# A decode layer on one core: K loaded into V's buffer, the MLP's first layer moved, and w2 read in longer rows

## The chip, the cores and the metric

The kernel runs on one core of a Trainium2 chip. The metric is the device time of one execution in microseconds (us). A run counts as fast when it lies within 1.5% of its kernel's fastest. Each experiment was timed in five rounds beside the kernel before, on the same chip. The experiments ran in three groups on three chips, with medians of the kernel before of 113.86 (e1 to e4), 113.94 (e5, e6, e7, e9) and 113.86 us (e10 to e12), so medians of different groups compare to about 0.1 us.

## The reference, cut to what matters

One token (1 x 1024) passes through a layer norm, then through two branches that are added to it: attention with 32 query heads over the last 4096 keys of 4 key/value heads, and an MLP with a second layer norm.

```python
xn = _layernorm(x)
q  = xn @ wq                          # wq: 1024 x 4096, 8.39 MB
p  = softmax(q @ k[last 4096].T / sqrt(128))   # k: 4 x 4096 x 128, 4.19 MB
a  = (p @ v[last 4096]) @ wo          # v: 4.19 MB; wo: 4096 x 1024, 8.39 MB
h  = gelu(_layernorm(xn) @ w1 + b1)   # w1: 1024 x 3584, 7.34 MB
out = x + a + h @ w2 + b2             # w2: 3584 x 1024, 7.34 MB
```

All data are bf16. Each weight is used once for one token, so 39.85 MB must come out of memory whatever the kernel does.

## The kernel before

Three buffers are used twice: `bufA` holds wq and then wo; `bufB` holds K as it is loaded and then w1; `bufKV` holds the transposed K and V, and then w2. The sync engine issues all large loads in this order, with the waits that protect the buffers:

```python
wo_sb   = bufA[...]                                   # after wq, same bytes
w1_sb   = bufB[:, :].rearrange("p (kc c) -> p kc c", kc=DC)
knat_sb = bufB[:, 0:HKV * W].rearrange(...)           # K as loaded: w1's place
kt_sb   = bufKV[:, 0:HKV * W].rearrange(...)          # K transposed
v_sb    = bufKV[:, HKV * W:2 * HKV * W].rearrange(...)
w2_sb   = bufKV[:, 0:FC * 1024].rearrange(...)        # over K^T and V
...
# sync engine
for kc in range(DC):  sync.dma_start(out=wq_sb[:, kc], ...)            # L495
for g in range(HKV):  sync.dma_start(out=knat_sb[:, g], ...)           # L497
for g in range(HKV):  sync.dma_start(out=v_sb[:, g], ...)              # L502
sync.wait_ge(s_pe, mval("pe", f"kt{HKV * NCH - 1}"))   # last K transpose
for kc in range(DC):  sync.dma_start(out=w1_sb[:, kc], ...)            # L508
sync.wait_ge(s_pe, mval("pe", "qT"))
for gi in range(8):   sync.dma_start(out=wo_sb[:, 4*gi:4*gi+4, :], ...)# L511
sync.wait_ge(s_pe, mval("pe", "oT"))                   # attention's output
...                   sync.dma_start(out=w2_sb[:, c0:c0+gsz, :], ...)  # L518
```

TensorE works in this order: q (256 pairs of weight load and matmul, L354), K transposes (L373), scores (L389), transpose of the probabilities (L401), attention's output (L419), MLP's first layer (224 pairs, L445), projection by wo (64 matmuls of 512 columns, L459 and L462), and by w2 (56 such matmuls, L471 and L475). The last two stages have one column as weights and 512 columns of wo or w2 as moving data:

```python
for c in range(4 * gi, 4 * gi + 4):
    pe.matmul(acc_lo, lhsT=oT_bf[:, c:c+1], rhs=wo_sb[:, c, 0:512],    ...)
    pe.matmul(acc_hi, lhsT=oT_bf[:, c:c+1], rhs=wo_sb[:, c, 512:1024], ...)
```

## Time and profile before

| | before |
|---|---|
| time, median | 113.98 us (16 runs, 113.37 to 114.41; 113.9 in the six runs known before predicting) |
| span of the profiled run | 112.0 us |
| read | 39.86 MB |
| longest wait of the sync queue | 28.2 us, first w1 load |
| busy shares: TensorE / VectorE / ScalarE | 62% / 25% / 17% |

Two rows of the page of the kernel before. The span is cut into 40 slices of 2.8 us; the first row is the busy share of the DMA engines in tenths (9 is 90% or more), the second what they moved.

```profile
DMA  2999999999999991199999999999999999999910
GB/s 59 422 425 427 436 424 422 419 424 422 413 422 416 419 422 50 28 364 394 425 425 423 428 386 360 400 383 396 381 386 392 380 389 389 385 388 387 332 48 1
```

The engines are full, but for a hole: the two slices at 50 and 28 GB/s. The windowed view of the kernel before gives numbers: each line is a stretch of time, its length, the busy time of each engine (with instructions), the granted clock, the DMA share and the rate.

```profile
core 0: us, PE busy (x) PEld busy (x) DVE busy (x) ACT busy (x) POOL busy (x), PEclk, DMA share, GB/s
4.00:42.00 38.00, 17.14 (x348) 14.38 (x349) 12.83 (x48) 7.86 (x14) 0.00 (x0) 1.00 1.01 422
42.00:48.50 6.50, 5.27 (x51) 3.13 (x52) 4.49 (x7) 3.77 (x7) 0.00 (x0) 1.00 0.22 71
48.50:64.00 15.50, 9.13 (x151) 5.73 (x149) 6.58 (x14) 4.70 (x5) 0.00 (x0) 0.79 1.01 418
68.00:84.00 16.00, 13.07 (x234) 8.13 (x234) 1.10 (x6) 0.23 (x1) 0.00 (x0) 0.58 1.04 387
84.00:104.00 20.00, 17.24 (x78) 6.13 (x77) 0.00 (x0) 0.00 (x0) 0.00 (x0) 1.00 1.05 387
```

From 42.0 to 48.5 us the rate is 71 GB/s in place of 422. In the last two lines, wo and w2 in rows of 2 KB, it is 387 although the DMA share is full. The waits of the sync queue of the kernel before name the hole's cause (who waited, for whom, us in total, times, longest):

```profile
SPq L508 <- PE psum L373: 28.2, 1, 28.2
```

L508 is w1, L373 the last K transpose: w1 cannot land while K lies in `bufB`.

The timeline of TensorE in the kernel before, second half, shows when its stages ran (start, length, instruction, count, and idle time before with what ended it; "issue" means that it waited for nothing the profile shows):

```profile
60.08 1.03 PE L401 MATMUL psum<-Dbf,p_sb 32*128 32x32 bf16 x32 [5.92 <-DVE Dbf L276]
61.56 3.56 PE L419 MATMUL psum<-pT_bf,bufKV 128*128 128x8 bf16 x128 [0.45 <-DVE pT_bf L278]
...
68.28 3.55 PE L445 MATMUL psum<-y2T_bf,bufB 128*128 128x1 bf16 x128 [1.28 <-issue]
74.48 2.35 PE L445 MATMUL psum<-y2T_bf,bufB 128*128 128x1 bf16 x83 [2.65 <-issue]
76.76 0.59 PE L459 MATMUL psum<-bufA,oT_bf 128*1 128x512 bf16 x1
```

TensorE stands idle for 5.9 us before L401 (softmax), then does the MLP's first layer (L445). In the w2 stage it waits for loads; from its waits after 76 us:

```profile
PE psum L471 <- DMA bufKV<-in_B_w_dram: 3.3, 5, 0.8
```

### The profile page before, as it was taken

The numbers are of one execution on the slowest core, as the hardware profiler recorded it, in microseconds if no ns is written. First come the engines' busy times: TensorE is split into PE (matmuls) and PEld (weight loads), VectorE is DVE, ScalarE is ACT, GpSimd is POOL, SyncE is SP. The second block draws the span as 40 slices with busy tenths as digits, with TensorE's granted clock in tenths as the row PEclk, the third lists the DMA queues.
The fourth block names the chain that finished last, engine by engine and source line by source line (L and its number), as shares of the span: only waits on it lengthen the run. The fifth ranks groups of instructions, "written<-read, shape, count | busy, mean of one in ns | idle before, by whom it ended". The sixth has DMA issues, their size and how long they took to land.

```text
span 112.0 us, 2144 instructions
## 1 busy us (share of the span) xinstructions
PE 69.4 (62%) x930; PEld 40.5 (36%) x930; DVE 27.7 (25%) x104; ACT 18.6 (17%) x29; POOL 0.2 (0%) x4
## 2 busy tenths in 40 slices
PE   0032000049678889699303986639999998777981
PEld 0021000049576656344003946635333333222320
DVE  3655300000027888567504000003000000000002
ACT  1201600000006677600293000000000000000002
POOL 0000000000000000000000000000000000000000
PEclk9999999999999999999975555555599999999999
DMA  2999999999999991199999999999999999999910
GB/s 59 422 425 427 436 424 422 419 424 422 413 422 416 419 422 50 28 364 394 425 425 423 428 386 360 400 383 396 381 386 392 380 389 389 385 388 387 332 48 1
DMA packets 11468, 39.99 MB, mean 357 GB/s; under 512 B 703, under 2 KB 707, under 8 KB 9412
## 3 DMA queue, kind: packets, MB, share of 16 engines
q1 hardware_dynamic: 11394, 39.85, 90.3%
q8 instruction: 7, 0.11, 0.4%
q10 hardware_dynamic: 66, 0.01, 0.1%
q14 instruction: 1, 0.01, 0.0%
HBM read 39.86 MB, written 0.00 MB: 356 GB/s over the span
## 4 chain that ended last, share of the span: by engine, by line
SPq 41%; DMA 29%; PE 15%; DVE 8%; issue 3%; ACT 1%; DVEq 0%
SPq L511 24%; DMA bufA<-in_A_wq_dram 17%; SPq L518 15%; DMA bufKV<-in_B_w_dram 12%; DVE bufKV L263 8%; PE psum L354 6%; PE psum L373 4%; PE psum L389 3%; SPq L495 3%; PE psum L471 1%; PE psum L475 1%; ACT bufKV L305 1%; ACT out_row L331 0%; ACT out_row L332 0%; DVEq L27 0%
## 5 line engine op out<-in xcount | busy, mean ns | idle before, releaser
L354 PE MATMUL psum<-xnT_bf,bufA 128*128 128x1 bf16 x256 | 7.1, 165 | 14.4 <-DMA bufA<-in_A_wq_dram 12.7
L459 PE MATMUL psum<-bufA,oT_bf 128*1 128x512 bf16 x32 | 13.6, 424 | 0.0
L305 ACT ACTIVATE bufKV<-psum 128x512 bf16<-128x512 f32 x16 | 9.6, 597 | 23.8 <-PE psum L373 23.7
L462 PE MATMUL psum<-bufA,oT_bf 128*1 128x512 bf16 x32 | 13.4, 419 | 0.0
L373 PE MATMUL psum<-I,bufB 128*128 128x128 bf16 x128 | 12.3, 246 | 1.5 <-DVE bufKV L263 0.5
L471 PE MATMUL psum<-bufKV,h_bf 128*1 128x512 bf16 x28 | 10.6, 378 | 3.4 <-DMA bufKV<-in_B_w_dram 3.3
L354 PEld LDWEIGHTS psum<-xnT_bf,bufA 128*128 128x128 bf16 x256 | 7.0, 104 | 14.5 <-issue 14.5
L263 DVE CAST bufKV<-psum 128x512 bf16<-128x512 f32 x16 | 11.1, 691 | 2.1 <-PE psum L373 0.8
L475 PE MATMUL psum<-bufKV,h_bf 128*1 128x512 bf16 x28 | 10.6, 379 | 0.0
L373 PEld LDWEIGHTS psum<-I,bufB 128*128 128x128 bf16 x128 | 8.7, 109 | 5.0 <-DVE bufKV L263 3.8
L445 PE MATMUL psum<-y2T_bf,bufB 128*128 128x1 bf16 x224 | 6.4, 165 | 3.9 <-issue 3.9
L290 DVE CAST out_row<-psum 1x256 bf16<-1x256 f32 x1 | 0.4, 411 | 30.9 <-PE psum L471 30.9
L445 PEld LDWEIGHTS psum<-y2T_bf,bufB 128*128 128x128 bf16 x224 | 6.2, 104 | 4.1 <-issue 4.1
L389 PE MATMUL psum<-bufKV,qT_pad 128*32 128x512 bf16 x32 | 7.1, 379 | 0.8 <-ACT bufKV L305 0.8
L270 DVE TENSOR_REDUCE pmax<-psum 32x1 f32<-32x512 f32 x8 | 5.4, 679 | 2.8 <-PE psum L389 2.8
L471 PEld LDWEIGHTS psum<-bufKV,h_bf 128*1 128x1 bf16 x28 | 2.3, 83 | 9.6 <-DMA bufKV<-in_B_w_dram 6.8
L331 ACT ACTIVATE out_row<-psum 1x256 bf16<-1x256 f32 x1 | 0.4, 374 | 31.6 <-PE psum L475 31.6
L256 DVE CAST qT_pad<-psum 128x8 bf16<-128x8 f32 x4 | 0.7, 166 | 20.0 <-PE psum L354 19.9
L313 ACT ACTIVATE p_sb<-psum,smw 32x2048 bf16<-32x2048 f32 x2 | 3.9, 1958 | 8.4 <-DVE smw L272 8.3
L459 PEld LDWEIGHTS psum<-bufA,oT_bf 128*1 128x1 bf16 x32 | 2.9, 91 | 5.1 <-issue 1.8
L401 PE MATMUL psum<-Dbf,p_sb 32*128 32x32 bf16 x32 | 1.0, 183 | 5.9 <-DVE Dbf L276 5.9
L462 PEld LDWEIGHTS psum<-bufA,oT_bf 128*1 128x1 bf16 x32 | 2.9, 90 | 4.9 <-issue 1.5
(74 smaller groups left out, 33.5 us busy)
## 6 DMA issues: line engine op xcount, KB each, us to landing
bufA<-in_A_wq_dram SPq DMA_DIRECT2D x8, 1024.0 KB, 12.1
bufA<-in_A_wo_dram SPq DMA_DIRECT2D x8, 1024.0 KB, 15.4
bufB<-in_B_w_dram SPq DMA_DIRECT2D x8, 896.0 KB, 10.5
bufKV<-in_B_w_dram SPq DMA_DIRECT2D x5, 1024.0 KB, 14.3
bufB<-in_A_k_cache_dram SPq DMA_DIRECT2D x4, 1024.0 KB, 24.6
bufKV<-in_A_v_cache_dram SPq DMA_DIRECT2D x4, 1024.0 KB, 28.1
bufKV<-in_B_w_dram SPq DMA_DIRECT2D x2, 768.0 KB, 13.3
bufKV<-in_B_w_dram SPq DMA_DIRECT2D x1, 512.0 KB, 12.3
```

Of the source, the lines that this page charges most:

```text
L263: lambda g=g, cb=cb, b=b: vec.tensor_copy(kt_sb[:, g, 512 * cb:512 * (cb + 1)], psum[:, SA[b]:SA[b] + 512]),
L305: lambda g=g, cb=cb, b=b: act.activation(kt_sb[:, g, 512 * cb:512 * (cb + 1)], psum[:, SA[b]:SA[b] + 512], _AF.Copy),
L354: lambda h=h, kc=kc: pe.matmul(qT_psum[:, h:h + 1], lhsT=wq_sb[:, kc, h * P:(h + 1) * P], rhs=xnT_bf[:, kc:kc + 1], start=(kc == 0), stop= ...
L373: lambda g=g, c=c, b=b, i=i: pe.matmul(psum[:, SA[b] + P * i:SA[b] + P * (i + 1)], lhsT=knat_sb[:, g, c, :], rhs=I128[:, :], start=True, s ...
L389: lambda g=g, t=t: pe.matmul(psum[0:HQ, 512 * t:512 * (t + 1)], lhsT=qT_pad[:, g, :], rhs=kt_sb[:, g, 512 * t:512 * (t + 1)], start=(g == ...
L445: lambda c=c, kc=kc, last=last: pe.matmul(hT_psum[:, c:c + 1], lhsT=w1_sb[:, kc, c * P:(c + 1) * P], rhs=y2T_bf[:, kc:kc + 1], start=False ...
L459: lambda c=c: pe.matmul(acc_lo, lhsT=oT_bf[:, c:c + 1], rhs=wo_sb[:, c, 0:512], start=False, stop=False)
L462: lambda c=c: pe.matmul(acc_hi, lhsT=oT_bf[:, c:c + 1], rhs=wo_sb[:, c, 512:1024], start=False, stop=False)
L471: lambda c=c, last=last: pe.matmul(acc_lo, lhsT=h_bf[:, c:c + 1], rhs=w2_sb[:, c, 0:512], start=False, stop=last),
L475: lambda c=c, last=last: pe.matmul(acc_hi, lhsT=h_bf[:, c:c + 1], rhs=w2_sb[:, c, 512:1024], start=False, stop=last),
L511: sync.dma_start(out=wo_sb[:, 4 * gi:4 * gi + 4, :], in_=wo_dram[:, 4 * gi:4 * gi + 4, :],).then_inc(s_wo[gi], 16)
L518: sync.dma_start(out=w2_sb[:, c0:c0 + gsz, :], in_=w2_dram[:, c0:c0 + gsz, :],).then_inc(s_w2[gi], 16)
```

## The change

The intent: close the hole, read w2 in longer rows, and fill TensorE's idle time during softmax. K goes where V will be; w1 follows K without a wait; V waits for the transposes, on GpSimd's queue. w2 (and with it w1's columns and b1) is permuted so that a partition reads four consecutive rows; the matching weights of the MLP's first layer are then read with a step of four elements. The diff, cut to its core:

```diff
-    b1_dram = B_b1.rearrange("(c p) -> c p", p=P)
+    b1_dram = B_b1.rearrange("(cc m) -> cc m", m=512)
-    w2_dram = B_w2.rearrange("(c p) n -> p c n", p=P)
+    w2_dram = B_w2.rearrange("(cc p j) n -> p cc j n", p=P, j=4)
-    W2G = [4, 4, 4, 4, 4, 3, 3, 2]
+    W2G = [4, 4, 4, 4, 2, 2, 2, 2, 2, 2]
-    knat_sb = bufB[:, 0:HKV * W].rearrange("p (g u d) -> p g u d", g=HKV, u=NU)
+    knat_sb = v_sb
+    w1_j = bufB[:, :].rearrange("p (kc cc m j) -> p kc cc m j", kc=DC, m=P, j=4)
 ... # the exp of the probabilities in three pieces (512, 1536, 2048), not two
 ... # TensorE: MLP's first layer now between the scores and the probabilities' transpose
-                        lhsT=w1_sb[:, kc, c * P:(c + 1) * P],
+                        lhsT=w1_j[:, kc, c // 4, :, c % 4],
 ... # sync engine: wq, K, then
+            for i in range(DC):
+                sync.dma_start(out=w1_sb[:, i], in_=w1_dram[:, i]).then_inc(s_w1[i], 16)
             sync.wait_ge(s_pe, mval("pe", "qT"))
 ...         # wo, then after oT: w2 in the new groups
+        @block.gpsimd
+        def _(pool):
+            pool.wait_ge(s_pe, mval("pe", f"kt{HKV * NCH - 1}"))
+            for i in range(HKV):
+                pool.dma_start(out=v_sb[:, i], in_=A_v_cache[...]).then_inc(s_v[i], 16)
```

More of the change, by code (lines that the diff above doesn't have):

```diff
@@ L107, in bass_parallel_sum__sliding_block_cached__mixer_channel_mlp__decode_kernel @@
     xb2 = sb([2, 512], bf16)
-    b1_28 = sb([FC, P], bf16)
+    b1_28 = sb([FC // 4, 512], bf16)
     J32 = sb([32, 32], bf16)
@@ L148, in bass_parallel_sum__sliding_block_cached__mixer_channel_mlp__decode_kernel @@
     s_v = [nc.alloc_semaphore(f"s_v{i}") for i in range(HKV)]
-    s_wo = [nc.alloc_semaphore(f"s_wo{i}") for i in range(HQ // 4)]
-    W2G = [4, 4, 4, 4, 4, 3, 3, 2]
+    WOG = 4
+    s_wo = [nc.alloc_semaphore(f"s_wo{i}") for i in range(HQ // WOG)]
+    W2G = [4, 4, 4, 4, 2, 2, 2, 2, 2, 2]
     s_w2 = [nc.alloc_semaphore(f"s_w2{i}") for i in range(len(W2G))]
@@ L159, in bass_parallel_sum__sliding_block_cached__mixer_channel_mlp__decode_kernel @@
     w1_sb = bufB[:, :].rearrange("p (kc c) -> p kc c", kc=DC)
-    knat_sb = bufB[:, 0:HKV * W].rearrange("p (g u d) -> p g u d", g=HKV, u=NU)
+    w1_j = bufB[:, :].rearrange("p (kc cc m j) -> p kc cc m j", kc=DC, m=P, j=4)
     kt_sb = bufKV[:, 0:HKV * W].rearrange("p (g c) -> p g c", g=HKV)
     v_sb = bufKV[:, HKV * W:2 * HKV * W].rearrange("p (g u d) -> p g u d", g=HKV, u=NU)
+    knat_sb = v_sb
     w2_sb = bufKV[:, 0:FC * 1024].rearrange("p (c n) -> p c n", c=FC)
+    w2_j = bufKV[:, 0:FC * 1024].rearrange("p (cc j n) -> p cc j n", cc=FC // 4, j=4)
     PS_XT = 3584
@@ L184, in bass_parallel_sum__sliding_block_cached__mixer_channel_mlp__decode_kernel @@
     hT_psum = psum[:, PS_HT:PS_HT + FC]
+    hT_j = hT_psum.rearrange("p (cc j) -> p cc j", j=4)
+    b1_j = b1_28[:, :].rearrange("p (m j) -> p m j", j=4)
     oT_psum = psum[:, PS_OT:PS_OT + HQ]
@@ L272, in vec_prog @@
         E.op(lambda: vec.tensor_scalar(smw[:, 1:2], smw[:, 0:1], -scale, None, _ALU.mult), name="negb")
-        E.wait("act", "exp1")
-        E.op(lambda: vec.tensor_reduce(smw[:, 2:3], esum8[:, 0:2], _AX.X, _ALU.add))
+        E.wait("act", "exp2")
+        E.op(lambda: vec.tensor_reduce(smw[:, 2:3], esum8[:, 0:3], _AX.X, _ALU.add))
         E.op(lambda: vec.reciprocal(smw[:, 3:4], smw[:, 2:3]))
@@ L310, in act_prog @@
         E.wait("dve", "negb")
-        for sx in range(2):
+        for sx, (e0, e1) in enumerate(((0, 512), (512, 2048), (2048, 4096))):
             E.op(
-                lambda sx=sx: act.activation(
-                    p_sb[:, 2048 * sx:2048 * (sx + 1)],
-                    psum[0:HQ, 2048 * sx:2048 * (sx + 1)],
+                lambda sx=sx, e0=e0, e1=e1: act.activation(
+                    p_sb[:, e0:e1],
+                    psum[0:HQ, e0:e1],
                     _AF.Exp,
@@ L347, in pe_prog @@
         E.wait("dve", "var2")
-        for kc in range(DC):
-            E.wait_sem(s_wq[kc], 16)
+        for i in range(DC):
+            E.wait_sem(s_wq[i], 16)
         for h in range(HQ):
@@ L397, in pe_prog @@
                 )
+        E.wait("act", "exp0")
+        E.wait("dve", "y2")
+        E.wait_sem(s_b1, 16)
+        for i in range(DC):
+            E.wait_sem(s_w1[i], 16)
+        for j in range(4):
+            E.op(
+                lambda j=j: pe.matmul(
+                    hT_j[:, :, j], lhsT=b1_j[:, :, j], rhs=I128[0:FC // 4, 0:FC // 4], start=(j == 0), stop=False
+                )
+            )
+        for c in range(FC):
+            for kc in range(DC):
+                last = (c == FC - 1) and (kc == DC - 1)
+                E.op(
+                    lambda c=c, kc=kc, last=last: pe.matmul(
+                        hT_psum[:, c:c + 1],
+                        lhsT=w1_j[:, kc, c // 4, :, c % 4],
+                        rhs=y2T_bf[:, kc:kc + 1],
+                        start=False,
+                        stop=last,
+                    ),
+                    name=("hT" if last else None),
+                )
         E.wait("dve", "D")
@@ L434, in pe_prog @@
             )
-        E.wait("act", "exp0")
-        E.wait("dve", "y2")
-        E.wait_sem(s_b1, 16)
-        for kc in range(DC):
-            E.wait_sem(s_w1[kc], 16)
-        E.op(lambda: pe.matmul(hT_psum, lhsT=b1_28[0:FC, :], rhs=I128[0:FC, 0:FC], start=True, stop=False))
-        for c in range(FC):
-            for kc in range(DC):
-                last = (c == FC - 1) and (kc == DC - 1)
-                E.op(
-                    lambda c=c, kc=kc, last=last: pe.matmul(
-                        hT_psum[:, c:c + 1],
-                        lhsT=w1_sb[:, kc, c * P:(c + 1) * P],
-                        rhs=y2T_bf[:, kc:kc + 1],
-                        start=False,
-                        stop=last,
-                    ),
-                    name=("hT" if last else None),
-                )
         E.wait("dve", "oTbf")
-        for gi in range(HQ // 4):
+        for gi in range(HQ // WOG):
             E.wait_sem(s_wo[gi], 16)
-            for c in range(4 * gi, 4 * gi + 4):
+            for c in range(WOG * gi, WOG * gi + WOG):
                 E.op(
@@ L493, in _ @@
         def _(sync):
-            for kc in range(DC):
-                sync.dma_start(out=wq_sb[:, kc], in_=wq_dram[:, kc]).then_inc(s_wq[kc], 16)
-            for g in range(HKV):
+            for i in range(DC):
+                sync.dma_start(out=wq_sb[:, i], in_=wq_dram[:, i]).then_inc(s_wq[i], 16)
+            for i in range(HKV):
                 sync.dma_start(
-                    out=knat_sb[:, g],
-                    in_=A_k_cache[0, g, W0:SK, :].rearrange("(q u) d -> q u d", q=P),
-                ).then_inc(s_k[g], 16)
-            for g in range(HKV):
-                sync.dma_start(
-                    out=v_sb[:, g],
-                    in_=A_v_cache[0, g, W0:SK, :].rearrange("(q u) d -> q u d", q=P),
-                ).then_inc(s_v[g], 16)
-            sync.wait_ge(s_pe, mval("pe", f"kt{HKV * NCH - 1}"))
-            for kc in range(DC):
-                sync.dma_start(out=w1_sb[:, kc], in_=w1_dram[:, kc]).then_inc(s_w1[kc], 16)
-            sync.wait_ge(s_pe, mval("pe", "qT"))
-            for gi in range(HQ // 4):
-                sync.dma_start(
-                    out=wo_sb[:, 4 * gi:4 * gi + 4, :],
-                    in_=wo_dram[:, 4 * gi:4 * gi + 4, :],
+                    out=knat_sb[:, i],
+                    in_=A_k_cache[0, i, W0:SK, :].rearrange("(q u) d -> q u d", q=P),
+                ).then_inc(s_k[i], 16)
+            for i in range(DC):
+                sync.dma_start(out=w1_sb[:, i], in_=w1_dram[:, i]).then_inc(s_w1[i], 16)
+            sync.wait_ge(s_pe, mval("pe", "qT"))
+            for gi in range(HQ // WOG):
+                sync.dma_start(
+                    out=wo_sb[:, WOG * gi:WOG * gi + WOG, :],
+                    in_=wo_dram[:, WOG * gi:WOG * gi + WOG, :],
                 ).then_inc(s_wo[gi], 16)
@@ L517, in _ @@
             for gi, gsz in enumerate(W2G):
+                cc, j = c0 // 4, c0 % 4
                 sync.dma_start(
-                    out=w2_sb[:, c0:c0 + gsz, :],
-                    in_=w2_dram[:, c0:c0 + gsz, :],
+                    out=w2_j[:, cc, j:j + gsz, :],
+                    in_=w2_dram[:, cc, j:j + gsz, :],
                 ).then_inc(s_w2[gi], 16)
@@ L526, in _ @@
             sync.wait_ge(s_out, 16)
+        @block.gpsimd
+        def _(pool):
+            pool.wait_ge(s_pe, mval("pe", f"kt{HKV * NCH - 1}"))
+            for i in range(HKV):
+                pool.dma_start(
+                    out=v_sb[:, i],
+                    in_=A_v_cache[0, i, W0:SK, :].rearrange("(q u) d -> q u d", q=P),
+                ).then_inc(s_v[i], 16)
         @block.vector
```

## The prediction

> **What bounds it now.** The kernel reads 39.85 MB; the DMA engines are the limit. The page's slices show them full except for one hole. By the windowed view the rate is 419 to 425 GB/s from 4 to 41 us (wq and K, rows of 8 KB). Between 42.0 and 48.5 us only 0.46 MB moved, 1.1 us' worth at 423 GB/s: 5.4 us are lost. The cause is in the sync queue's waits: the first w1 load waits 28.2 us for the last K transpose (46.3 us), because w1 lands in K's buffer, and nothing else was left to load. Later the rate is 421 to 427 with w1 (7 KB rows), but only 382 to 390 GB/s from 68 to 106 us, with wo and w2 in 2 KB rows, at a full DMA share. The last w2 groups land at 107.1 us; 10 matmuls of 0.215 us follow, then copies and the output, to 112.0 us. The chain of waits agrees: 41% sync queue's issues, 29% DMA.
>
> **What the change does.**
> 1. K goes to V's future place, so w1 has its buffer alone and is issued right behind K. V waits for the last transpose, on GpSimd's queue, while w1 (until about 49 us: 19.9 MB at 423 GB/s from 2.1 us) and wo (free from the q matmuls' end, 32.7 us) keep the engines busy. The hole vanishes: -5.4 us.
> 2. w2 is read in rows of 8 KB (four loads) and 4 KB (six). The Trainium skill, "DMA: Bandwidth & Descriptors", section Why small descriptors are slow, states a fixed cost per packet; the trace agrees in direction, 423 GB/s at 7 to 8 KB against 386 at 2 KB. Its 7.34 MB take about 17.6 in place of 19.0 us (estimate from these rates): -1.4 us.
> 3. Last groups of two chunks: 4 to 8 matmuls after the last landing, not 10: -0.4 to -1.2 us.
> 4. The MLP's first layer moves ahead of the probabilities' transpose and loads weights with a step of four elements (8 bytes). Its 224 pairs now cost 6.4 us plus 3.9 us of issue gaps. "SBUF — State Buffer", section Door 1, states that two hits per 16-byte line suffice; no strided weight load is in this trace. I expect 6 to 13 us, from about 56 us on.
> 5. V shares the engines with wo from 46 us; by estimate it lands at 60 to 68 us, and attention's output is ready at 68 to 72 us. Then w2 may be issued; wo keeps the engines busy until about 81 us, so some 9 us of slack cover 4 and 5.
>
> **Sum.** 113.9 - 5.4 - 1.4 - 0.8 = 106.3; plus 0.2 for two queues: 106.5 us, range 105.0 to 109.0. Chances: faster by over 2% 0.94, within 2% 0.04, slower 0.02.
>
> **What would show it.** No slice with DMA share under 9 before the tail; w1 landed at about 50 us; w2 moving above 405 GB/s; V landed before 70 us; attention's output before 78 us; last w2 landing near 100 us; under 1.8 us of matmuls after it.
>
> **What would make it wrong.** Strided loads of 100 ns or more per pair (22 us), or V starved behind the deep sync queue: attention's output after 81 us, and a new hole of several us before w2. Or the second half's rate is limited by something other than row size: then w2 gains nothing, 108 us.

## The result, and the profile after

| | before | after |
|---|---|---|
| time, median | 113.98 us (16 runs) | 106.45 us (8 runs, 106.27 to 106.70) |
| ratio | | 0.9343, 95% interval 0.9325 to 0.9362 |
| span of the profiled run | 112.0 us | 104.5 us |

Ratios are the mean time of one kernel's fast runs over that of the other's of the same rounds, so not quite the ratio of the medians quoted. All outputs are right.

The page's DMA rows of the changed kernel, slices of 2.6 us:

```profile
DMA  4999999999999999999999999999999999999910
GB/s 57 396 430 420 433 414 427 427 423 414 423 411 415 429 412 420 428 396 430 417 405 410 413 417 383 387 388 384 389 387 392 419 411 430 412 406 411 370 72 1
```

The hole is gone. The windowed view of the changed kernel (stretches chosen for the same stages; wo moves in the fourth, w2 in the fifth):

```profile
4.00:42.00 38.00, 17.15 (x348) 14.39 (x349) 12.82 (x48) 7.86 (x14) 0.00 (x0) 1.00 1.01 422
42.00:48.50 6.50, 5.27 (x51) 3.14 (x52) 4.49 (x7) 3.77 (x7) 1.86 (x4) 1.00 1.02 418
48.50:64.00 15.50, 12.62 (x229) 9.18 (x226) 5.90 (x13) 4.45 (x6) 0.36 (x1) 0.79 1.02 409
64.00:80.00 16.00, 13.83 (x216) 7.92 (x214) 1.99 (x8) 0.82 (x2) 0.00 (x0) 0.56 1.05 387
82.00:98.00 16.00, 16.00 (x76) 6.22 (x74) 0.00 (x0) 0.00 (x0) 0.00 (x0) 1.00 1.02 414
```

The second stretch went from 71 to 418 GB/s, w2 from 387 to 414; wo, whose 2 KB rows were not touched, stayed at 387. Among the sync queue's waits w1 (now L512) no longer appears. The only one left that holds back a load is wo's (L515), 3.4 us for q, with other loads in flight:

```profile
SPq L515 <- PE psum L359: 3.4, 1, 3.4
```

TensorE's timeline in the changed kernel:

```profile
56.10 0.29 PE L410 MATMUL psum<-I,b 7*128 7x7 bf16 x4 [1.94 <-ACT p_sb L318]
56.33 5.91 PE L418 MATMUL psum<-y2T_bf,bufB 128*128 128x1 bf16 x173
63.18 1.86 PE L418 MATMUL psum<-y2T_bf,bufB 128*128 128x1 bf16 x51 [0.95 <-issue]
64.97 1.03 PE L430 MATMUL psum<-Dbf,p_sb 32*128 32x32 bf16 x32
66.45 1.32 PE L448 MATMUL psum<-pT_bf,bufKV 128*128 128x8 bf16 x44 [0.45 <-DVE pT_bf L283]
...
72.74 0.59 PE L469 MATMUL psum<-bufA,oT_bf 128*1 128x512 bf16 x1
```

The MLP's first layer (L418) now fills the softmax wait, and the projections start at 72.7 us, 4 us earlier than before. TensorE's waits for w2 in the changed kernel, after 76 us, and the end of its chain of waits (start, length, what):

```profile
PEld psum L481 <- DMA bufKV<-in_B_w_dram: 1.4, 3, 0.7
PE psum L481 <- DMA bufKV<-in_B_w_dram: 0.2, 1, 0.2
```

```profile
81.04 19.90 DMA bufKV<-in_B_w_dram
100.94 0.04 issue
100.98 0.38 PE psum L481
101.36 0.22 PE psum L485
101.58 0.22 PE psum L481
101.79 0.23 PE psum L485
```

Here is the reading that the prediction had not made. The chain ends in a w2 load (100.94 us), but from 72.7 us to the end TensorE's matmuls (PE) stood idle for a load only once, for 0.2 us; its weight loads (PEld) waited three times, 1.4 us in all, mostly while earlier matmuls still ran. By the spacing of the matmuls' starts TensorE lost about 0.6 us to loads. Its 120 projection matmuls are 28 us of back-to-back work, since each takes 0.215 us, and 0.43 us for the first dozen, at half clock. So the kernel now has two limits that end within about 1 us of each other: the DMA engines, and TensorE counted from attention's output.

When a load's data are complete can be read from the trace's landing records, in which each load completes sixteen times, once per DMA engine. The last completion of some loads, in us from the span's start:

```
                     before   after
last w1 load          66.25   52.66
last V load           44.09   65.59
last wo load          89.59   83.39
last w2 load but one 107.13   99.71
last w2 load         108.41  100.94
end of span          112.0   104.5
```

The last landing moved by 7.47 us and the span by 7.5: the gain is there, ahead of the last landing.

### The profile page after: what moved, and what is told of

Its sections match the earlier page's. It is cut to its first block, busy times and chain, and to the rows that moved or that the text cites. A ratio compares the mean times of both kernels' runs of the same rounds, so it can differ in the third digit from the quotient of the medians.

```text
span 104.5 us, 2154 instructions
## 1 busy us (share of the span) xinstructions
PE 70.6 (68%) x933; PEld 42.6 (41%) x933; DVE 27.7 (26%) x104; ACT 18.9 (18%) x31; POOL 2.4 (2%) x8
## 4 chain that ended last, share of the span: by engine, by line
DMA 38%; PE 30%; SPq 12%; DVE 10%; issue 6%; ACT 2%; DVEq 0%
DMA bufKV<-in_B_w_dram 19%; DMA bufA<-in_A_wq_dram 19%; SPq L523 8%; DVE bufKV L268 8%; PE psum L418 7%; PE psum L359 7%; PE psum L394 7%; PE psum L378 4%; PE psum L448 4%; SPq L505 3%; ACT p_sb L318 1%; DVE pT_bf L283 1%; DVE pmax L275 1%; ACT bufKV L310 1%; PE psum L481 1%
## 5 line engine op out<-in xcount | busy, mean ns | idle before, releaser
L469 PE MATMUL psum<-bufA,oT_bf 128*1 128x512 bf16 x32 | 13.8, 430 | 0.0
L472 PE MATMUL psum<-bufA,oT_bf 128*1 128x512 bf16 x32 | 13.7, 427 | 0.0
L378 PE MATMUL psum<-I,bufKV 128*128 128x128 bf16 x128 | 12.3, 246 | 1.4 <-DVE bufKV L268 0.5
L378 PEld LDWEIGHTS psum<-I,bufKV 128*128 128x128 bf16 x128 | 8.7, 109 | 4.9 <-DVE bufKV L268 3.8
L418 PE MATMUL psum<-y2T_bf,bufB 128*128 128x1 bf16 x224 | 7.8, 172 | 0.9 <-issue 0.9
L418 PEld LDWEIGHTS psum<-y2T_bf,bufB 128*128 128x128 bf16 x224 | 7.6, 118 | 1.1 <-issue 1.0
L318 ACT ACTIVATE p_sb<-psum,smw 32x512 bf16<-32x512 f32 (+2 forms) x3 | 4.2, 1389 | 8.4 <-DVE smw L277 8.3
L448 PE MATMUL psum<-pT_bf,bufKV 128*128 128x8 bf16 x128 | 3.7, 168 | 2.2 <-issue 1.7
L394 PEld LDWEIGHTS psum<-bufKV,qT_pad 128*32 128x32 bf16 x32 | 3.0, 97 | 4.5 <-DVE bufKV L268 0.9
```

What stands on the lines that cost most here:

```text
L378: lambda g=g, c=c, b=b, i=i: pe.matmul(psum[:, SA[b] + P * i:SA[b] + P * (i + 1)], lhsT=knat_sb[:, g, c, :], rhs=I128[:, :], start=True, s ...
L394: lambda g=g, t=t: pe.matmul(psum[0:HQ, 512 * t:512 * (t + 1)], lhsT=qT_pad[:, g, :], rhs=kt_sb[:, g, 512 * t:512 * (t + 1)], start=(g == ...
L418: lambda c=c, kc=kc, last=last: pe.matmul(hT_psum[:, c:c + 1], lhsT=w1_j[:, kc, c // 4, :, c % 4], rhs=y2T_bf[:, kc:kc + 1], start=False, ...
L448: lambda g=g, u=u: pe.matmul(oT_psum[:, G * g:G * (g + 1)], lhsT=v_sb[:, g, u, :], rhs=pT_bf[:, HQ * u + G * g:HQ * u + G * (g + 1)], star ...
L469: lambda c=c: pe.matmul(acc_lo, lhsT=oT_bf[:, c:c + 1], rhs=wo_sb[:, c, 0:512], start=False, stop=False)
L472: lambda c=c: pe.matmul(acc_hi, lhsT=oT_bf[:, c:c + 1], rhs=wo_sb[:, c, 512:1024], start=False, stop=False)
```

## The experiments

Theory A: only the DMA engines limit; the other parts of the change ride along. Theory B: TensorE's work behind attention's output is a second limit of nearly the same length, so that moving the MLP's first layer matters. In the texts below, "Theory A" and "Theory B" are these.

| run | what | median us | ratio to before (95%) | last w2 landing us |
|---|---|---|---|---|
| changed kernel | | 106.45 | 0.9343 (0.9325, 0.9362) | 100.94 |
| e1 | buffers and order alone | 108.88 | 0.9567 (0.9535, 0.9599) | 102.18 |
| e6 | rows and groups alone | 112.50 | 0.9884 (0.9862, 0.9906) | 107.08 |
| e2 | changed, natural rows | 107.90 | 0.9487 (0.9456, 0.9517) | 102.37 |
| e3 | changed, MLP late | 110.50 | 0.9709 (0.9672, 0.9746) | 101.02 |
| e4 | changed, V on sync queue | 106.46 | 0.9361 (0.9328, 0.9394) | 100.90 |
| e10 | changed, all w2 loads 8 KB rows | 107.06 | 0.9396 (0.9373, 0.9419) | 100.70 |
| e5 | changed, projections turned round | 107.20 | 0.9419 (0.9399, 0.9439) | 102.13 |
| e7 | e5 with the MLP late | 107.35 | 0.9425 (0.9408, 0.9443) | 102.22 |
| e9 | e5 with wo in 4 KB rows | 106.88 | 0.9380 (0.9361, 0.9399) | 101.89 |
| e11 | changed, 128 idle pairs | 106.63 | 0.9346 (0.9323, 0.9370) | 101.10 |
| e12 | changed, 256 idle pairs | 107.89 | 0.9462 (0.9439, 0.9486) | 102.43 |

### e1: buffers and order alone

```diff
 # on the kernel before
-    knat_sb = bufB[...]
+    knat_sb = v_sb
 ... # w1 issued behind K without a wait; V on GpSimd's queue; all else as before
```

> Step 1 alone on the kernel before (K in V's place, w1 right behind K, V on GpSimd's queue); rows, groups and the place of the MLP's first layer stay as before. Theory A (only the DMA engines limit): the hole goes, last w2 landing at about 101.7 us, 10 matmuls after it, about 108.5 us, ratio 0.952. Theory B (TensorE's work after attention's output is a second limit of nearly the same length): the MLP's first layer, still behind attention, lets the output projections start only at 75 to 77 us; their 120 matmuls take 28 us whatever lands, so TensorE ends near 104.5 us, hardly waits for any w2 landing, and the time is 109 us or more.

The last landing fell from 108.41 to 102.18 us, by 6.2 us: that is what taking out the hole was worth at the last landing. The span fell by only 4.9 us. The answer on TensorE's waits after 76 us has no line for a load at all: with the MLP's first layer still behind attention, the projections started at 76.47 us and ran through to 104.7 us, 2.5 us past the last landing. Theory B's account holds, though the time of 108.88 us lies just under its "109 us or more"; Theory A's account falls, though its time of 108.5 us was close.

### e6: rows and groups alone

```diff
 # on the kernel before: b1, w1 and w2 permuted, W2G = [4, 4, 4, 4, 2, 2, 2, 2, 2, 2]
 # K, V, w1 in their old buffers and order; the MLP's first layer in its old place
```

> Steps 2 and 3 alone on the kernel before: permuted w1, b1 and w2 rows and the ten w2 groups, but K, V and w1 in their old buffers and order and the MLP's first layer in its old place. The hole of 5.4 us stays. w2 moves at 407 to 423 GB/s: last landing near 105.7 us in place of 107.1, 4 matmuls after it: 111.4 to 112.0 us, ratio 0.977 to 0.983. Under Theory B TensorE is close behind: the strided loads make its projections start 1.4 us later, so it should hardly wait for w2 any more.

A miss in size: ratio 0.988, not 0.977 to 0.983. The landing moved by 1.33 us as the rows' sum says, but from 108.41, not from the 107.1 us that I had read as the last landing, and the smaller groups gave nothing. The part about Theory B was a miss too: TensorE's projections started at 77.4 us, only 0.6 us later than before, and it still waited 1.9 us for w2, so it did not limit here.

### e2: the changed kernel with natural rows

```diff
-    w2_dram = B_w2.rearrange("(cc p j) n -> p cc j n", p=P, j=4)
+    w2_dram = B_w2.rearrange("(c p) n -> p c n", p=P)
-                        lhsT=w1_j[:, kc, c // 4, :, c % 4],
+                        lhsT=w1_sb[:, kc, c * P:(c + 1) * P],
 ... # b1 likewise; the ten groups stay
```

> The changed kernel with w1, b1 and w2 back in natural order: w2 in 2 KB rows (same ten groups), contiguous weight loads in the MLP's first layer. Row-size theory: w2 moves at 385 to 390 GB/s again, last landing 1.2 to 1.6 us later than 100.9, time 107.5 to 108.0, ratio 0.944 to 0.950. Rival (the rate of the second half has another cause than rows, or TensorE hides it): ratio within 0.002 of the changed kernel's 0.934. The 224 pairs at contiguous weights should take 27 to 28 ns each in place of 33.8.

The last landing is 1.43 us later, the time 1.45 us. The windowed view of e2, in the stretches where wo and then w2 move:

```profile
64.00:80.00 16.00, 13.48 (x230) 7.95 (x229) 1.99 (x8) 0.82 (x2) 0.00 (x0) 0.55 1.05 386
82.00:98.00 16.00, 16.00 (x76) 6.23 (x74) 0.00 (x0) 0.00 (x0) 0.00 (x0) 1.00 1.05 386
```

At 2 KB w2 moves at 386 GB/s, as wo does; in the changed kernel it moved at 414. The time follows the row size. The contiguous pairs took 4.77 us for 176 of them, 27.1 ns each; the strided pairs of the changed kernel, in the same place, 5.91 us for 173, or 34.2 ns by the timeline (33.8 by the chain of waits, which I had quoted). By these rates the step of four costs about 1.5 us over 224 pairs. But the stage hardly grew shorter without it. TensorE's timeline in e2:

```profile
56.73 4.77 PE L412 MATMUL psum<-y2T_bf,bufB 128*128 128x1 bf16 x176
63.85 1.44 PE L412 MATMUL psum<-y2T_bf,bufB 128*128 128x1 bf16 x48 [2.35 <-issue]
65.22 1.03 PE L424 MATMUL psum<-Dbf,p_sb 32*128 32x32 bf16 x32
```

From its first pair to the next stage it took 8.5 us, against 8.6 us with the step (56.33 to 64.97 us in the changed kernel): the faster pairs were followed by a longer "issue" wait, 2.35 us in place of 0.95. What such a wait is, the section on e5, e7 and e9 takes up.

### e3: the changed kernel with the MLP's first layer back in its old place

```diff
 # TensorE's order, in words
-  scores, MLP's first layer, probabilities' transpose, attention's output, projections
+  scores, probabilities' transpose, attention's output, MLP's first layer, projections
```

> The changed kernel with only the MLP's first layer moved back behind attention's output. My prediction gave this stage 9 us of slack (Theory A): then nothing changes, 106.5 us. Theory B: the output projections start about 3 to 5 us later (75.5 to 78 us in place of 72.7) and TensorE never waits for w2; the time rises by 2.5 to 4 us, to 109 to 110.5 us, although w2 lands at about the same time or earlier.

4.05 us slower than the changed kernel, with the last w2 load at the same time within 0.1 us. The windowed view of e3 at its end:

```profile
core 0: us, PE busy (x) PEld busy (x) DVE busy (x) ACT busy (x) POOL busy (x), PEclk, DMA share, GB/s
96.00:100.00 4.00, 4.00 (x20) 1.51 (x18) 0.00 (x0) 0.00 (x0) 0.00 (x0) 1.00 0.87 346
100.00:106.00 6.00, 6.00 (x28) 2.19 (x26) 0.17 (x1) 0.00 (x0) 0.00 (x0) 1.00 0.03 10
```

For the last 6 us the DMA engines are all but idle and TensorE busy without a gap: it started the projections at 77.58 us and ended at 106.0. Of the 9 us of slack that I gave to this stage some 0.8 us exist: a start 4.84 us later cost 4.05 us. It is worse than e1, which also has the MLP late: there the weights were contiguous and the projections started 1.1 us earlier.

### e4: V on the sync queue

```diff
-            pool.wait_ge(...kt31); pool.dma_start(out=v_sb[:, i], ...)   # GpSimd
+            sync.wait_ge(...kt31); sync.dma_start(out=v_sb[:, i], ...)   # behind w1, ahead of wo
```

> The changed kernel with V issued by the sync queue, behind w1 and ahead of wo, at the same wait for the last K transpose. If GpSimd's queue matters only by letting V be issued while something else is in flight: w1 is in flight until about 49 us, V is issued at 46.4, so no hole: 106.5 us within 0.4, V lands at about 59 to 60 us. If a separate queue is needed to keep the engines full: a hole of 1 to 3 us at 46 to 50 us and 107.5 us or more.

No difference: 106.46 us, and no hole. V landed at 61.8 us in place of 65.6, a little later than I expected. This agrees with the Trainium skill, "DMA: Bandwidth & Descriptors", section Issuing engines are not separate DMA queues: loads issued by different engines run on the same 16 DMA engines and interleave. The order of issue closed the hole, and the second queue did not add to it.

### e10: w2 in seven loads, all with 8 KB rows

```diff
-    W2G = [4, 4, 4, 4, 2, 2, 2, 2, 2, 2]
+    W2G = [4, 4, 4, 4, 4, 4, 4]
```

> The changed kernel with w2 in seven groups of four chunks, all rows 8 KB, in place of four of 8 KB and six of 4 KB. The last six groups moved at about 407 GB/s, 8 KB rows at 420: the last landing comes some 0.3 us earlier, but 8 matmuls follow it (1.7 us) in place of 4 (0.9 us). Prediction from the sum: 0.3 to 0.8 us slower, 106.8 to 107.3 us. If the smaller last groups were worth nothing: 106.2 us.

As the sum said: the last landing came 0.24 us earlier, but eight matmuls followed it, and the time rose by 0.6 us. The small last groups of the change earn their shorter rows.

### e5, e7 and e9: turned-round projections

If TensorE is a second limit, halving its projection work should make its place in the chain irrelevant, and leave room for longer rows of wo.

```diff
-  pe.matmul(acc_lo, lhsT=oT_bf[:, c:c+1], rhs=wo_sb[:, c, 0:512], ...)      # 120 matmuls of 512 columns
+  pe.matmul(accT[:, n:n+1], lhsT=wo_sb[:, c, n*P:(n+1)*P], rhs=oT_bf[:, c:c+1], ...)   # 480 pairs
+  # accT (128 x 8) is copied to bf16 and turned back by one matmul with the identity
```

> The changed kernel with the two output projections turned round: blocks of the weights are the stationary operand (480 pairs of 128x128 weights and one moving column, at the 27 to 28 ns per pair seen in the other stages, 13.4 us) in place of 120 matmuls of 512 columns (28 us); the [128 x 8] result is turned back by one small matmul. Everything else as changed. If the DMA engines and TensorE tie in the changed kernel as I read it, nothing large is gained, since the last w2 load still lands near 100.9 us: 105.8 to 106.6 us. If TensorE alone set the end: 104.5 us or less.

> The same turned-round projections, with the MLP's first layer back behind attention (the place that cost 4 us in the run before). Theory B (that cost was TensorE's 28 us behind attention's output): with only 13.4 us there the late place costs nothing, 105.8 to 106.8 us. Rival (a late MLP delays the DMA issues or something else): 109 us or more again.

> Turned-round projections, and wo read in rows of 4 KB: attention's output is computed in two halves of 64 strided columns of V (256 pairs in place of 128) and put back by four small copies. Row-size theory: wo's 8.39 MB move at about 407 in place of 388 GB/s, 1.0 us less, so 104.8 to 105.5 us. Rival (TensorE or attention's later output limits): no gain over the run with turned-round projections alone.

e7 settles the question of place: with the turned-round projections, moving the MLP late costs 0.15 us (107.35 against 107.20) in place of 4.05. So the cost of the late place was TensorE's work behind attention's output, as Theory B says. But e5 itself was 0.75 us slower than the changed kernel, a miss: its last w2 load landed at 102.13 us, 1.2 us later, though nothing about the large loads was edited. e7 missed its range for the same reason (102.22 us). e9 read wo at 408 GB/s in place of 387 and won 0.3 us over e5, less than the 1.0 us expected. Its loads were ahead of e5's by more than that up to the fifth w2 load (94.71 us against 95.82), but by only 0.24 us at the last; between 94 and 96 us they moved at 315 GB/s. Why they lost it there was not tested.

What delayed the loads? The sixteen completions of the last w2 load, each as its lead over the last one (first, eighth, fifteenth), and the times at which 16 KB packets of the instruction queue began, from the trace's landing and packet records:

```
              first   8th  15th   instruction packets at (us)
changed       -1.85 -1.35 -0.09   29.0 35.2 45.0 60.8 67.1 73.2 82.5
e5            -3.02 -2.08 -1.20   29.1 35.3 45.2 60.8 67.0 73.4 79.6 85.8 91.9 (100.4)
```

In e5 fifteen engines were done 1.2 us before the sixteenth. The load that landed at 90.8 us had no such gap (fifteenth completion 0.08 us ahead), the next, at 94.5 us, had it (1.22 us). Between them, at 91.9 us, lies the ninth instruction packet; such a packet holds an engine for 1.0 to 1.1 us. TensorE's timeline in e5 shows the other side, its waits for instructions, between runs of exactly 128 pairs (256 instructions of 64 bytes are 16 KB):

```profile
75.78 3.57 PE L463 MATMUL psum<-oT_bf,bufA 128*128 128x1 bf16 x128 [2.22 <-issue]
82.25 2.42 PE L463 MATMUL psum<-oT_bf,bufA 128*128 128x1 bf16 x85 [2.90 <-issue]
```

The Trainium skill, "Runtime: NRT & Kernel Launch", section Instruction fetch mechanics, states the 16 KiB block of 256 instructions, and calls the cost of crossing a block boundary mostly hidden. Here it was not hidden: packets came about 6.2 us apart, TensorE stood still for 2 to 3 us at a time, and one DMA engine of sixteen fell behind. The theory that the ninth packet does the harm was then tested by itself.

### e11 and e12: more instructions, nothing else

```diff
+        for _ in range(128):      # e12: 256; while TensorE waits for wq, from about 12 us
+            pe.matmul(psum[:, 3700:3701], lhsT=I128[:, :], rhs=xnT_bf[:, 0:1], start=True, stop=True)
```

> The changed kernel with 128 idle pairs (128x128 weights, one column, result unused) put on TensorE at 13 us, where it waits for wq until 23.8 us. Fetch theory (from the runs with turned-round projections): each 16 KB packet of TensorE's instructions holds one of the 16 DMA engines for 1.1 us; the first eight hit engines with slack, the ninth hits one that is already last and delays every later load by about 1.2 us. One packet more, eight in all: no change, 106.5 us within 0.3. Rival (the turned-round runs landed late because of the way TensorE reads weights): no change either.

> The same with 256 idle pairs (7 us, still inside TensorE's wait for wq): nine packets. Fetch theory: the last w2 load lands about 1.2 us later, near 102.1 us, with 15 of its 16 completions about 1.2 us ahead of the last; 107.4 to 107.9 us. Rival: no change, 106.5 us.

The instruction queue's lines on the pages of the changed kernel, e11 and e12, in this order (packets, MB, share of 16 engines' span):

```profile
q8 instruction: 7, 0.11, 0.5%
```

```profile
q8 instruction: 8, 0.13, 0.5%
```

```profile
q8 instruction: 9, 0.15, 0.6%
```

Completions of the last w2 load, and the packets, as above:

```
              first   8th  15th   instruction packets at (us)
e11           -2.06 -0.91 -0.01   17.7 30.2 36.5 45.9 62.0 68.2 74.6 83.9
e12           -3.13 -2.13 -1.46   17.2 23.3 29.9 36.1 45.7 61.8 68.2 74.6 82.8
```

Eight packets cost nothing clear of noise (106.63 us); nine cost 1.44 us (107.89 us). In e12 the ninth packet began at 82.8 us. The load that landed at 80.8 us had its fifteenth completion 0.05 us ahead of the last, the load that landed at 85.0 us 1.57 us ahead, and all later loads kept that gap to the end. The rival, that the way of reading weights delayed the loads in e5, is not needed. One reservation: the early packets also delayed wq by some 0.7 us, and with it TensorE's projections by 1.2 us. But e11 had the same delay (projections from 74.0 us, 73.9 in e12) without the gap and without the cost, the chain of waits of e12 still ends in the w2 load that landed at 102.43 us, and the gap to its other fifteen completions is direct evidence. That the ninth packet returns to an engine that has had one already fits four kernels (e5, e7, e9, e12), but the trace does not name a packet's engine, so this stays an inference.

## Why the prediction was right, and where a step was off

The forecast was 106.5 us (105.0 to 109.0) and the median 106.45. The mechanism was right: the hole and the row size gave the gain. That the sum came within 0.05 us was luck: two of its terms erred in opposite directions, and the span could follow the loads only because the MLP's first layer was moved, which the prediction had taken for a side matter (5 below).

1. *The hole, -5.4 us.* Right in cause, too small in size: 6.2 us at the last landing (e1). The lost bytes account for 5.4. After the hole the rate was slow to recover, 398 GB/s from 48.5 to 53 us, about 0.3 us by estimate. And in both kernels with the hole (before, e6) the sixteen completions of the last load were on average 1.6 us ahead of the last one, without it (after, e1) 0.9 to 1.0: the slowest engine ended some 0.6 us further behind. This gap did not come with the hole itself. In the kernel before, the last w1 load, at 66.25 us, still had its fifteenth completion 0.01 us ahead of the last; the first wo load, at 70.33 us, 1.07 us. Between them, at 65.9 us, an instruction packet began: the same sign as in e12. In e6 it is 0.09 us at 64.13 us and 1.38 at 67.70, with a packet at 65.1. So the 0.6 us may be due to where a packet fell; no run tested this.
2. *Longer rows, -1.4 us.* Right: 1.43 us (e2 against the changed kernel) and 1.33 us (e6 against before), both at the last landing. The Trainium skill's statement in "DMA: Bandwidth & Descriptors", section Why small descriptors are slow, agrees in direction, 386 to 387 GB/s at 2 KB, 408 at 4 KB (wo in e9), 418 to 422 at 7 to 8 KB.
3. *Fewer matmuls after the last landing, -0.8 us.* This term was wrong: it was worth nothing against the kernel before. The last landing before was at 108.41 us, with 4 matmuls after it, not at 107.1 with 10. I took the last wait for a load (107.1 us) as the last landing, but the next load arrived while TensorE was still busy and so left no wait. From last landing to end of span it was 3.5 us before and 3.5 after. The small groups keep their worth only against large ones with the same rows (e10, 0.6 us).
4. *Strided weights, 6 to 13 us for the stage.* Right: 8.6 us, 34 ns per pair against 27 (e2). The SBUF page's statement that two hits per 16-byte line suffice was not borne out in full: a quarter more per pair. Whether the cost arises in SBUF or in TensorE's own reading of weights, no run tells. Without the step the stage took 8.5 us (e2), since waits for instructions filled the difference.
5. *V's landing at 60 to 68 us and attention's output at 68 to 72, "some 9 us of slack cover 4 and 5".* The times were right (65.6 and 71.9 us), and for the issue of w2 there was such slack. But the slack was counted to the wrong end. TensorE's 28 us of projections follow attention's output, and 72.7 + 28 is 101 us, the same as the last landing. e3 shows the price: a start 4.8 us later is 4.05 us of time. I had taken it that TensorE only follows the loads, from a kernel in which the DMA engines were later still.

Terms as measured: 6.2 (hole, e1) + 1.4 (rows) + 0 (groups) = 7.6 us at the last landing, against 7.47 observed; the 0.2 us allowed for two queues was not seen (e4, 106.46 us). That the span could follow is due to the move of the MLP's first layer: without it the buffers alone gave 4.9 us of span (e1), and buffers with rows 3.5 us (e3: 112.0 to 108.5). The exp in three pieces, also part of the change, was not tested alone. Of the listed signs, w1's landing came at 52.7, not 50 us; V's share of the engines explains only part, since it landed at 51.8 us in e4, where V comes behind it. The others held.

No experiment beat the changed kernel. Turned-round projections cost instruction packets, the gain of longer rows for wo (e9) was lost again before the last w2 load for a reason not tested, and larger w2 loads cost matmuls at the end.

## What to carry to other kernels

When a hole in the loads is closed, ask next what the other engine still has to do after the last point where it can start: add that work to its start time and compare it with the last landing, even if that engine only waits today. A wait shows only the landings that somebody stood waiting for, so read the last landing from the loads themselves. Before trading few long matmuls for many short ones, count instructions: in these runs 128 pairs made a 16 KB packet, and in the four kernels with nine packets or more the last loads landed 0.9 to 1.5 us later (101.89 to 102.43 us, against 100.94).

## What the Trainium skill lacked or had wrong

- "Runtime: NRT & Kernel Launch", Instruction fetch mechanics, calls the cost of a 16 KiB block boundary mostly hidden. With the load queues full, a packet held one DMA engine for 1.0 to 1.1 us, packets came 6.2 us apart, TensorE stalled for 0.9 to 2.9 us between runs of 128 pairs, and the ninth packet delayed every later load (e12: +1.44 us for 256 idle pairs; e11: nothing for 128).
- "SBUF — State Buffer", Door 1, lets one expect a stride of four bf16 elements to be free. With weights of 128 x 128 read so, a pair took 34 ns against 27 (e2); the whole stage took 8.6 us against 8.5. "TensorE: Matmul & The Clock Gate", Weight-path perf modes, allows packed or strided reads but gives no cost for the stride.
- "DMA: Bandwidth & Descriptors" has no table of rate against row size for full-size loads on trn2 from the sync queue. These runs show 386 to 387 GB/s at 2 KB, 408 at 4 KB, 418 to 422 at 7 to 8 KB.
- The same page's specifications give about 358 GB/s as the HBM limit of one core; further down the page says that this is roughly a core's part when both cores that share the memory stream. With one core running, these kernels held 422 GB/s for 38 us, which agrees with the 425 that the page measures for one core. So the page is not wrong, but its first table read alone misleads.
